# Preparing float64 weights: sign by a mask, remainders by an accumulating transfer, and a check for small weights

## The chip, the cores and the metric

One core of a Trainium2 chip runs the kernel. The metric is the device time of one execution in microseconds (us), less is better. The engines are PE (TensorE, with its weight loads, PEld), DVE (VectorE), ACT (ScalarE), POOL (GpSimd) and SP (SyncE, which here issues most transfers). Each engine runs its own list of instructions in order and waits on semaphores for the others.

## What is computed

A gated linear attention over 4 batches, 8 heads, 768 positions and a head width of 48, and on its output two matrix products with a piecewise quadratic between them:

```python
f = 1.0 / (1.0 + np.exp(-f_logit))
for t in range(S):
    state = f[:, :, t, :, None] * state + np.einsum('bhd,bhe->bhde', k[:, :, t], v[:, :, t])
    y[:, :, t] = np.einsum('bhd,bhde->bhe', q[:, :, t], state)
...
h = x @ w_in
g = np.where(pos, h, np.where(neg, 0.0, (h + beta) ** 2 / (4.0 * beta)))
return (g @ w_out).astype(np.float32)
```

x has 3072 rows and 384 columns, w_in is 384 by 2048 and w_out 2048 by 384. The two weight matrices arrive as float64; q, k, v and f_logit are float32.

## The kernel before

**Blocks.** The 768 positions are cut into NI = 6 row blocks of C = 128; with the 4 batches each block gives N = 512 columns to the products. The heads are taken in NP = 4 pairs. For each block and pair, `gate` makes running products of the forget gates (two scans on DVE), and `scores`, `outputs` and `states` make the attention by matmuls of the chunk and a state carried from block to block. `outputs` also splits its result into a rounded part (on ACT) and the remainder (on DVE), x; the fourth pair's part, y, reaches its place in x by six small transfers (`move`, x<-y in the profile).

**Units.** The products of a block are cut into NJ = 16 units of 128 columns of w_in. A unit is 9 matmuls in `mm_in` (L202), then act_1, act_2 on ACT, act_3 on DVE (L214), act_hi on ACT (L217, writes ghi), act_lo on DVE (L220, writes glo), and 9 matmuls in `mm_out` (L226). There are 96 units, numbered here from 0, so unit 16 is the first of the second block. Each product runs in three terms, of rounded parts and remainders: w_lo·hi, w_hi·hi and w_hi·lo.

**Weights.** They come as 24 pieces of 128 by 512 float64 (512 KB), in `order`: three pieces of w_in, three of w_out, and so on, as the first block's units need them; unit j of the first block needs the w_in pieces of its group of four units. The two 32-bit words of a number lie side by side in `raw`: lw and hw. `split_piece` shifts and joins them in `bits` to a float32 whose two highest bits are not yet right (L299, L302), reads the sign from the high word with two passes on ACT (L306, L307), takes the absolute value on ACT (L308), multiplies both on DVE (L309), rounds the result to w_hi on ACT (L311) and subtracts for w_lo on DVE (L312). There are four `raw` and two `bits` buffers. `outs`, where results are gathered for their transfer, lie in the `raw` buffers too.

**Order.** Nothing runs in program order: every piece of work is an `Op` with an engine, a cost from the table COST and what it depends on, and `Plan.order` simulates the engines to lay down one fixed order for each. At a moment it takes, of the work that is ready, what has the earliest latest start. A transfer issued by SP that has to wait holds every later one on SP's list. Where the plan sees PE idle for long, it puts in matmuls of zeros (`warm`, L280).

**The end.** A test of the first gates (ok, flag) decides whether a general path, slow and step by step, computes the whole again. With the inputs here it isn't taken.

Of the kernel before, what the change touches and what calls it, by code (L numbers as in the profile page):

```python
# [22 lines left out]
NI = S // C  # L23
# [4 lines left out]
N = B * C  # L28
HEADS = ((0, 48), (64, 112))

LEAST = 1e-15

NT = 3

W = 512
NW = DM * DF // (128 * W)
# [1 line left out]

HOP, LANDING, PER_KB, NEAR = 200, 2000, 3.0, 2000
COST = dict(mm=227, scores=1100, y0=1050, y=1850, states=500, turn=500, rows=317, scan=1145, dve=605, small=200, state=365,  # L40
            words=430, words2=690, act=710, copy=530, sig=540, issue=480, near=600, least=300)


class Op:
# [91 lines left out]
def gla_moe(ctx: ExitStack, tc: tile.TileContext, ff, kqd, f0, vv, wd, maskd, identd, gates, values, headsd, out):  # L136
    nc = tc.nc
    const = ctx.enter_context(tc.tile_pool(name="const", bufs=1))
# [3 lines left out]
    def tiles(count, shape, dtype, name):  # L142
        return [const.tile(shape, dtype, name=f"{name}_{k}") for k in range(count)]
# [7 lines left out]
    v = tiles(3, [C, B, 2, D], F32, "v")  # L151
# [27 lines left out]
    def wide(a):  # L179
        return a.rearrange("r b c -> r (b c)")  # L180
# [55 lines left out]
    add = plan.add  # L236

    def dma(dst, src, kb, *deps):
        return add("SP", "issue", lambda: nc.sync.dma_start(dst, src), *deps, kb=kb)
# [26 lines left out]

    def constants():
        nc.gpsimd.memset(ones_col, 1.0)
        for t, a in ((half, 0.5), (up, 512.0), (down, -512.0)):
            nc.gpsimd.memset(t, a)  # L270

    set_consts = add("POOL", 200, constants)
# [12 lines left out]
    piece = []  # L285
# [2 lines left out]
        order += [3 * q + n for n in range(3)] + [NW + 3 * q + n for n in range(3)]  # L288
    split = {}

    def split_piece(k):
        c = order[k]
        words = raw[k % 4].bitcast(U32).rearrange("p (n t) -> p n t", t=2)
        lw, hw = words[:, :, 0], words[:, :, 1]
        t = bits[k % 2]
        val, sign = t.bitcast(F32), hw.bitcast(F32)
        loaded = dma(raw[k % 4], wd[c], 8 * 128 * W / 1024, piece[k - 4] if k >= 4 else None)

        m = vec("words", lambda: nc.vector.tensor_scalar(  # L299
            out=t, in0=hw, scalar1=3, scalar2=0xC0000000, op0=ALU.logical_shift_left, op1=ALU.bitwise_xor),  # L300
            loaded, split[order[k - 2]] if k >= 2 else None)
        v = vec("dve", lambda: nc.vector.scalar_tensor_tensor(  # L302
            out=t, in0=lw, scalar=29, in1=t, op0=ALU.logical_shift_right, op1=ALU.bitwise_or), m)


        s = sca("words2", lambda: nc.scalar.activation(sign, sign, AF.Identity, bias=up), m, set_consts)  # L306
        s = sca("words2", lambda: nc.scalar.activation(sign, sign, AF.Sign, bias=down), s)  # L307
        v = sca("copy", lambda: nc.scalar.activation(val, val, AF.Abs), v)  # L308
        v = vec("dve", lambda: nc.vector.tensor_tensor(out=val, in0=val, in1=sign, op=ALU.mult), v, s)  # L309
        piece.append(v)  # L310
        h = sca("copy", lambda: nc.scalar.copy(w_hi[:, c], val), v)  # L311
        l = vec("dve", lambda: nc.vector.tensor_tensor(out=w_lo[:, c], in0=val, in1=w_hi[:, c].bitcast(F32), op=ALU.subtract), h)  # L312
        split[c] = [h, l]


    banks = {k: [] for k in range(6)}
# [217 lines left out]
        g["lo"] = vec("dve", lambda: act_lo(a, ghi[u % 2], glo[u % 2]), o, unit_out.get(u - 2))  # L534


    outs = [t.bitcast(F32)[:, 0:N] for t in raw[:3]]
    put = []

    def unit_2(u):  # L540
        i, j = divmod(u, NJ)
        hi, lo = ghi[u % 2], glo[u % 2]
        g = gs[u]
        need = [split[NW + c] for c in range(j * DM // W, ((j + 1) * DM - 1) // W + 1)]
        if j < NJ - 1:
            def first():
                mm_out(hi, lo, j, range(3), (0, 1))
                opened.update(bank=po[2], start=False)

            held = left.get(i - 1, [d for k in (3, 4, 5) for d in banks[k]]) if j == 0 else None  # L550
            add("PE", 6 * COST["mm"], first, g["hi"], need, held)
            unit_out[u] = add("PE", 3 * COST["mm"], lambda: mm_out(hi, lo, j, range(3), (2,)), g["lo"])
        else:
            left[i] = []
            for e in range(3):
                def last(e=e):
                    opened["bank"] = None
# [4 lines left out]
                o = (sca if e == 1 else vec)("dve", lambda e=e, t=t: copy_out(e, t), unit_out[u], put[-3] if len(put) >= 3 else [split[c] for c in order[-4:]])  # L562
                left[i].append(o)
                put.append(dma(out[i, :, e], t, 256, o))


    def prepare(n):
# [21 lines left out]
    for u in range(NI * NJ):  # L589
        unit_1(u)  # L590
        for kind, n in sorted(groups.get(u, [])):
            if kind == 0:
                prepare(n)
                if pairs[n][0] < NI - 1:
                    (transpose_tensor if pairs[n][0] < BY_TENSOR else transpose_rows)(n)
                scores(n)
            else:
                outputs(n)
                states(n)

        if 1 <= u < NI * NJ - 2:
            unit_2(u - 1)
    for u in range(NI * NJ - 3, NI * NJ):
        unit_2(u)

# [7 lines left out]
            o.emit()  # L613

    ok = const.tile([128, NI * NT * B + 1], F32, name="ok")
    nc.vector.tensor_scalar(out=ok[:, 1:], in0=f0s, scalar1=LEAST, scalar2=None, op0=ALU.is_ge)
    nc.vector.tensor_reduce(out=ok[:, 0:1], in_=ok[:, 1:], axis=mybir.AxisListType.X, op=ALU.min)
    ps = wide(pa[0])  # L620
    nc.tensor.matmul(ps[0:1, 0:1], ok[:, 0:1], ones_col, start=True, stop=True)
    flag = const.tile([1, 1], I32, name="flag")
    nc.vector.tensor_scalar(out=flag, in0=ps[0:1, 0:1], scalar1=127.5, scalar2=None, op0=ALU.is_lt)
    bad = nc.values_load(flag, min_val=0, max_val=1)
    with tc.If(bad > 0):
        heads = const.tile([R, 2], F32, name="heads")
        nc.sync.dma_start(heads, headsd)
        tmp = kq[:3]
# [115 lines left out]
```

## Time and profile before

| | us |
|---|---|
| median of 3 runs | 528.43 (527.32 to 530.09) |
| the profiled execution | 526.78, span 525.0 |
| granted TensorE clock, mean | 0.996 |
| PE / PEld busy | 505.8 / 404.8 |
| DVE busy | 386.0 |
| ACT busy | 274.4 |
| POOL busy | 11.9 |
| transfers | 41.67 MB, mean 79 GB/s |

The profile is of one execution. Its page gives the busy time of each engine, the span in 40 slices, the chain of work that ended last, and groups of instructions by line, engine, operation, tiles and shape, with their count, busy time, mean duration in ns, and the engine's idle time ahead of them with what ended it. A group reads "L299 DVE TENSOR_SCALAR bits<-raw 128x512 ... x24 | 10.0, 423 | 0.3": line 299, 24 instructions, 10.0 us, 423 ns each, 0.3 us idle ahead. In a timeline the first two numbers are the start and the duration in us. PE's busy time counts matmuls whose ends are modelled, so PE is not at its peak wherever it is called busy; its pace is read from the starts of its matmuls.

### The profile page before, as it was taken

Reading aid. Unit: us, or ns where it says so; the run is one execution under the profiler, and the core shown is the slowest. Engines: PE = TensorE matmul, PEld = TensorE weight load, DVE = VectorE, ACT = ScalarE, POOL = GpSimd, SP = SyncE. Lnnn points to the kernel's source line nnn. Section 1 sums busy time; section 2 is a strip of 40 time slices with the busy share of each in tenths; the row PEclk is TensorE's granted clock in tenths of the full one; section 3 lists DMA queues with packets and bytes.
Section 4 is the critical chain, followed back from the end, with each engine's and each line's share of the span. In section 5 each row is a group of like instructions: output and inputs, shape, how many; then the busy total and the mean of one; then the engine's idle time right before and its main releaser. Section 6 shows DMA issues by size and latency. Waiting matters only on the chain.

```text
span 525.0 us, 8314 instructions
## 1 busy us (share of the span) xinstructions
PE 505.8 (96%) x3245; PEld 404.8 (77%) x3253; DVE 386.0 (74%) x774; ACT 274.4 (52%) x447; POOL 11.9 (2%) x30
## 2 busy tenths in 40 slices
PE   8868999989999999999999999999999999999995
PEld 4546777868877778788888888888888888888884
DVE  7899999999999999997897698864544333433333
ACT  3578988986443444434534434434443444544442
POOL 1100000000000000000000000000000000000000
PEclk9989999999999999999999999999999999999999
DMA  8784454532322033222014112012200001100001
GB/s 294 252 295 140 138 190 151 186 117 46 100 76 66 2 95 87 70 60 73 21 56 96 60 57 77 1 55 63 66 24 1 1 0 32 61 1 0 1 0 64
DMA packets 17612, 41.67 MB, mean 79 GB/s; under 512 B 2976, under 2 KB 6560, under 8 KB 17568
## 3 DMA queue, kind: packets, MB, share of 16 engines
q1 hardware_dynamic: 16416, 38.73, 23.2%
q10 hardware_dynamic: 1152, 2.37, 1.9%
q8 instruction: 27, 0.44, 0.4%
q14 instruction: 17, 0.14, 0.1%
HBM read 31.63 MB, written 4.72 MB: 69 GB/s over the span
## 4 chain that ended last, share of the span: by engine, by line
PE 71%; DVE 21%; ACT 3%; issue 2%; DMA 1%; ACTq 0%; DVEq 0%
PE po L226 31%; PE ph L202 30%; PE pa L419 3%; PE pa L473 2%; PE pa L469 2%; DVE act L214 2%; DVE glo L220 2%; DVE kn L452 2%; DVE am L425 2%; DVE w_lo L312 2%; DVE bits L309 2%; DVE bits L302 2%; DVE bits L299 1%; DVE w L362 1%; DVE f L369 1%
## 5 line engine op out<-in xcount | busy, mean ns | idle before, releaser
L202 PE MATMUL ph<-x,w_hi 128*128 128x512 f32 x576 | 178.3, 391 | 0.0
L206 ACT ACTIVATE act<-ph,half 128x512 f32<-128x512 f32 x96 | 65.9, 687 | 132.7 <-PE ph L202 125.8
L202 PEld LDWEIGHTS ph<-x,w_hi 128*128 128x128 f32 x576 | 108.7, 189 | 22.9
L226 PE MATMUL po<-ghi,w_lo 128*128 128x512 f32 x288 | 116.2, 403 | 4.0 <-ACT ghi L217 4.0
L214 DVE SCALAR_TENSOR_TENSOR act<-ph,act 128x512 f32<-128x512 f32 x96 | 65.9, 686 | 69.6 <-ACT act L209 69.0
L202 PE MATMUL ph<-x,w_lo 128*128 128x512 f32 x288 | 113.4, 394 | 3.4 <-DMA x<-y 3.4
L226 PE MATMUL po<-ghi,w_hi 128*128 128x512 f32 x288 | 112.5, 390 | 0.0
L217 ACT CAST ghi<-act 128x512 fp32r<-128x512 f32 x96 | 59.5, 620 | 80.0 <-DVE act L214 79.8
L226 PE MATMUL po<-glo,w_hi 128*128 128x512 f32 x288 | 83.5, 391 | 0.5 <-DVE glo L220 0.5
L220 DVE TENSOR_TENSOR glo<-act,ghi 128x512 fp32r<-128x512 f32 x96 | 66.0, 687 | 24.1 <-ACT ghi L217 23.1
L226 PEld LDWEIGHTS po<-ghi,w_lo 128*128 128x128 f32 x288 | 54.0, 188 | 20.3 <-ACT ghi L217 7.7
L202 PEld LDWEIGHTS ph<-x,w_lo 128*128 128x128 f32 x288 | 54.4, 189 | 15.5 <-DMA x<-y 3.9
L226 PEld LDWEIGHTS po<-glo,w_hi 128*128 128x128 f32 x288 | 53.6, 188 | 13.5 <-DVE glo L220 2.3
L209 ACT ACTIVATE act<-act 128x512 f32<-128x512 f32 x96 | 60.7, 632 | 2.8
L226 PEld LDWEIGHTS po<-ghi,w_hi 128*128 128x128 f32 x288 | 54.1, 188 | 10.3
L452 DVE STREAM_TRANSPOSE kn<-kq 32x128 f32<-32x128 f32 x192 | 58.1, 303 | 2.9
L425 DVE TENSOR_TENSOR am<-pa,mask 128x512 f32<-128x512 f32 x43 | 29.4, 686 | 19.3 <-PE pa L419 15.1
L468 PE MATMUL pa<-am,v 128*64 128x128 f32 x184 | 35.5, 279 | 1.1 <-DVE am L425 0.6
L469 PE MATMUL pa<-am,v 128*48 128x128 f32 x184 | 34.5, 277 | 0.5 <-DVE am L425 0.5
L472 PE MATMUL pa<-kq,dbd 112*64 112x128 f32 x160 | 30.6, 272 | 0.0
L473 PE MATMUL pa<-kq,dbd 112*48 112x128 f32 x160 | 30.6, 272 | 0.0
L419 PEld LDWEIGHTS pa<-kq 48*128 48x128 f32 x344 | 21.3, 187 | 6.6 <-issue 5.6
(79 smaller groups left out, 478.5 us busy)
## 6 DMA issues: line engine op xcount, KB each, us to landing
raw<-in_w SPq DMA_DIRECT2D x24, 512.0 KB, 4.4
kq<-in_kq SPq DMA_DIRECT2D x18, 512.0 KB, 3.7
v<-in_v SPq DMA_DIRECT2D x24, 192.0 KB, 4.0
out_y<-raw SPq DMA_DIRECT2D x18, 256.0 KB, 2.2
f<-in_f SPq DMA_DIRECT2D x16, 256.5 KB, 2.7
kq<-kq SPq DMA_DIRECT2D x18, 64.2 KB, 2.3
kq<-kq ACTq DMA_DIRECT2D x18, 64.2 KB, 2.7
x<-y SPq DMA_DIRECT2D x18, 64.0 KB, 3.6
```

The source lines that it names most:

```text
L202: nc.tensor.matmul(ps, w_in(part, j, kt), xt[:, kt, t], start=(n == 0), stop=(n == 8))
L206: nc.scalar.activation(a, ps, AF.Relu, bias=half, scale=0.5)
L209: nc.scalar.activation(a, a, AF.Square)
L214: nc.vector.scalar_tensor_tensor(out=a, in0=ps, scalar=1.0, in1=a, op0=ALU.max, op1=ALU.min)
L217: nc.scalar.copy(hi, a)
L220: nc.vector.tensor_tensor(out=lo, in0=a, in1=hi.bitcast(F32), op=ALU.subtract)
L226: nc.tensor.matmul(po[e], w_out(part, j, e), g, start=(j == 0 and n == 0), stop=(j == NJ - 1 and n == 2))
L419: nc.tensor.matmul(ps[:, b], kt[a:z, B - 1 - b], qt[a:z, b], start=True, stop=True)
L425: o = vec("dve", lambda t=t, ps=ps: nc.vector.tensor_tensor(out=t, in0=ps, in1=mask.rearrange("u (o t) -> u o t", o=1).broadcast_to([C, B, ...
L452: nc.vector.transpose(kn[n % 2][u:u + 32, :, r:r + 32], src[:, :, u:u + 32])
L469: nc.tensor.matmul(ps[64:R, m], vb[:, D:], ms[1][:, m], start=True, stop=first)
L473: nc.tensor.matmul(ps[64:R, m], dt[:, m, 64:R], qt[:, m], start=False, stop=True)
```

## The change

A piece is now put together with three DVE instructions: shift and mask (so that the two highest bits are zero), join with the low word, join with the two highest bits of the high word. That gives the float32 at once, with its sign, for a weight in float32's range; one too small for it comes out wrong (SMALL, 2^-15, is the bound for the high word when that is read as a float32). The two sign passes, the absolute value and the multiplication go. ACT writes w_lo as minus the rounded value, and POOL issues a transfer that adds the value to it in place: w_lo is the remainder. w_hi is made as before. `raw` has three buffers, `bits` four.

For such weights, `small_piece` loads all 24 pieces a second time into the third `raw` buffer, one after the other, and reduces each to its least absolute high word (DVE, into ok). `test` joins that with the test of the first gates, inside the plan and ahead of the last three units' second halves, and the general path, if taken, splits the weights again with the old sign. The results' buffers, `outs`, move into the first two `raw` buffers. COST gains the issue on POOL and loses the sign pass.

```diff
-    raw = tiles(4, [128, W], I64, "raw")
-    bits = tiles(2, [128, W], U32, "bits")
+    raw = tiles(3, [128, W], I64, "raw")
+    bits = tiles(4, [128, W], U32, "bits")
...
     def split_piece(k):
+
         c = order[k]
...
-        loaded = dma(raw[k % 4], wd[c], 8 * 128 * W / 1024, piece[k - 4] if k >= 4 else None)
+        loaded = dma(raw[k % 3], wd[c], 8 * 128 * W / 1024, piece[k - 3] if k >= 3 else None)
+
 
         m = vec("words", lambda: nc.vector.tensor_scalar(
-            out=t, in0=hw, scalar1=3, scalar2=0xC0000000, op0=ALU.logical_shift_left, op1=ALU.bitwise_xor),
-            loaded, split[order[k - 2]] if k >= 2 else None)
+            out=t, in0=hw, scalar1=3, scalar2=0x3FFFFFF8, op0=ALU.logical_shift_left, op1=ALU.bitwise_and),
+            loaded, split[order[k - 4]] if k >= 4 else None)
         v = vec("dve", lambda: nc.vector.scalar_tensor_tensor(
             out=t, in0=lw, scalar=29, in1=t, op0=ALU.logical_shift_right, op1=ALU.bitwise_or), m)
-
-
-        s = sca("words2", lambda: nc.scalar.activation(sign, sign, AF.Identity, bias=up), m, set_consts)
-        s = sca("words2", lambda: nc.scalar.activation(sign, sign, AF.Sign, bias=down), s)
-        v = sca("copy", lambda: nc.scalar.activation(val, val, AF.Abs), v)
-        v = vec("dve", lambda: nc.vector.tensor_tensor(out=val, in0=val, in1=sign, op=ALU.mult), v, s)
+        v = vec("dve", lambda: nc.vector.scalar_tensor_tensor(
+            out=t, in0=hw, scalar=0xC0000000, in1=t, op0=ALU.bitwise_and, op1=ALU.bitwise_or), v)
         piece.append(v)
+
+        n = sca("copy", lambda: nc.scalar.activation(w_lo[:, c], val, AF.Copy, scale=-1.0), v)
+        l = add("POOL", "swdge", lambda: nc.gpsimd.dma_start(w_lo[:, c], val, accum_op=ALU.add), n, near=True)
         h = sca("copy", lambda: nc.scalar.copy(w_hi[:, c], val), v)
-        l = vec("dve", lambda: nc.vector.tensor_tensor(out=w_lo[:, c], in0=val, in1=w_hi[:, c].bitcast(F32), op=ALU.subtract), h)
         split[c] = [h, l]
+
+    seen = []
+
+    def small_piece(c):
+
+        loaded = dma(raw[2], wd[c], 8 * 128 * W / 1024, seen[-1:] or piece[-3:])
+        seen.append(vec("dve", lambda: nc.vector.tensor_reduce(
+            out=ok[:, 1 + NG + c:2 + NG + c], in_=words_of(raw[2])[1].bitcast(F32), axis=mybir.AxisListType.X, op=ALU.min,
+            apply_absolute_value=True), loaded))
...
-    outs = [t.bitcast(F32)[:, 0:N] for t in raw[:3]]
+    outs = [raw[0].bitcast(F32)[:, 0:N], raw[0].bitcast(F32)[:, N:2 * N], raw[1].bitcast(F32)[:, 0:N]]
...
+    def test():
+        def compare():
+            nc.vector.tensor_scalar(out=ok[:, 1:1 + NG], in0=f0s, scalar1=LEAST, scalar2=None, op0=ALU.is_ge)
+            nc.vector.tensor_scalar(out=ok[:, 1 + NG:], in0=ok[:, 1 + NG:], scalar1=SMALL, scalar2=None, op0=ALU.is_ge)
+            nc.vector.tensor_reduce(out=ok[:, 0:1], in_=ok[:, 1:], axis=mybir.AxisListType.X, op=ALU.min)
+
+        ps = wide(pa[0])
+        o = vec(500, compare, seen, [c["pf"] for c in gates_of])
+        o = add("PE", 500, lambda: nc.tensor.matmul(ps[0:1, 0:1], ok[:, 0:1], ones_col, start=True, stop=True), o, banks[0], set_consts)
+        vec("small", lambda: nc.vector.tensor_scalar(out=flag, in0=ps[0:1, 0:1], scalar1=127.5, scalar2=None, op0=ALU.is_lt), o)
...
     for k in range(2 * NW):
         split_piece(k)
+    for c in range(2 * NW):
+        small_piece(c)
```

The plan lays down a new order. In what follows the lines of the changed kernel have numbers of their own: L306, L309 and L311 are the three instructions of a piece, L216 and L222 are act_3 and act_lo, L512 is the remainder of x or y, L325 the reduction.

DVE's list just ahead of the first unit, before the change. L299, L302, L309 and L312 belong to pieces, L425 masks scores, L481 on y is what the x<-y transfers of the first block wait for:

```order
L481 TENSOR_TENSOR x_88<-pa_110,x_88 112x512
L309 TENSOR_TENSOR bits_100<-bits_100,raw_96 128x512
L425 TENSOR_TENSOR am_78<-po_115,mask 128x512
L425 TENSOR_TENSOR am_79<-po_116,mask 128x512
L309 TENSOR_TENSOR bits_99<-bits_99,raw_97 128x512
L312 TENSOR_TENSOR w_lo<-bits_100,w_hi 128x512
L299 TENSOR_SCALAR bits_100<-raw_98 128x512
L302 SCALAR_TENSOR_TENSOR bits_100<-raw_98,bits_100 128x512
L312 TENSOR_TENSOR w_lo<-bits_99,w_hi 128x512
L481 TENSOR_TENSOR y_90<-po_117,y_90 112x512
```

The same place in the changed kernel, from the end of the third piece on; the gate's scans are w (L393) and f (L400):

```order
L311 SCALAR_TENSOR_TENSOR bits_100<-raw_97,bits_100 128x512
L512 TENSOR_TENSOR x_88<-pa_111,x_88 112x512
L393 SCALAR_TENSOR_TENSOR w<-f_66,ones 128x512
L456 TENSOR_TENSOR am_78<-po_116,mask 128x512
L456 TENSOR_TENSOR am_79<-po_117,mask 128x512
L306 TENSOR_SCALAR bits_101<-raw_95 128x512
L309 SCALAR_TENSOR_TENSOR bits_101<-raw_95,bits_101 128x512
L311 SCALAR_TENSOR_TENSOR bits_101<-raw_95,bits_101 128x512
L396 TENSOR_SCALAR end_77<-w 128x4
L399 RECIPROCAL rec<-end_77 128x4
L400 SCALAR_TENSOR_TENSOR f_66<-f_66,rec 128x512
L512 TENSOR_TENSOR y_90<-po_118,y_90 112x512
```

A fourth piece stood ahead of y's remainder in both. It came with a `raw` buffer of its own (raw_98) and now comes with the first one's (raw_95), and the next gate's two scans have moved ahead of y's remainder.

SP's list at that time, before; the first four pieces' loads are already issued, and raw_95 is the fifth piece's:

```order
L239 DMA kq_68<-in_kq 128x1024
L244 DMA kq_71<-kq_69 16x1028
L244 DMA kq_71<-kq_70 16x1028
L239 DMA v_73<-in_v 128x384
L239 DMA kq_69<-in_kq 128x1024
L239 DMA raw_95<-in_w 128x512
L239 DMA kq_70<-in_kq 128x1024
```

And now, where raw_95 is the fourth piece's:

```order
L241 DMA kq_68<-in_kq 128x1024
L246 DMA kq_71<-kq_69 16x1028
L246 DMA kq_71<-kq_70 16x1028
L241 DMA v_73<-in_v 128x384
L241 DMA kq_69<-in_kq 128x1024
L241 DMA raw_95<-in_w 128x512
L241 DMA kq_70<-in_kq 128x1024
L241 DMA raw_96<-in_w 128x512
L241 DMA raw_97<-in_w 128x512
```

The load of the first buffer's second piece stands where it stood, behind the kq load, but it is the fourth piece's now. Two more loads (raw_96, raw_97) follow behind the next kq load, ahead of a v load that stood ahead of them.

DVE's list some 60 units later in the changed kernel, where the checks stand (nothing of the kind stood there before):

```order
L216 SCALAR_TENSOR_TENSOR act_86<-ph_114,act_86 128x512
L222 TENSOR_TENSOR glo_93<-act_86,ghi_91 128x512
L325 TENSOR_REDUCE ok<-raw_97 128x1
L216 SCALAR_TENSOR_TENSOR act_87<-ph_115,act_87 128x512
L222 TENSOR_TENSOR glo_94<-act_87,ghi_92 128x512
L325 TENSOR_REDUCE ok<-raw_97 128x1
L216 SCALAR_TENSOR_TENSOR act_86<-ph_114,act_86 128x512
L222 TENSOR_TENSOR glo_93<-act_86,ghi_91 128x512
L325 TENSOR_REDUCE ok<-raw_97 128x1
L216 SCALAR_TENSOR_TENSOR act_87<-ph_115,act_87 128x512
```

A reduction (L325) stands ahead of each of three act_3 (L216) here, and waits there for its load. The 24 reductions stand between the act_3 of unit 31 and that of unit 74; stretches with one per unit are up to six units long and hold a pair of the attention.

More of the change, by code (lines that the diff above doesn't have):

```diff
@@ L31 @@
 LEAST = 1e-15
+SMALL = 2.0 ** -15
 NT = 3
@@ L268, in constants @@
         nc.gpsimd.memset(ones_col, 1.0)
-        for t, a in ((half, 0.5), (up, 512.0), (down, -512.0)):
+        for t, a in ((half, 0.5), (up, 768.0), (down, -768.0)):
             nc.gpsimd.memset(t, a)
@@ new lines, in split_again @@
+    def split_again(c):
+        lw, hw = words_of(raw[0])
+        t = bits[0]
+        val, sign = t.bitcast(F32), hw.bitcast(F32)
+        nc.sync.dma_start(raw[0], wd[c])
+        nc.vector.tensor_scalar(out=t, in0=hw, scalar1=3, scalar2=0x3FFFFFF8, op0=ALU.logical_shift_left, op1=ALU.bitwise_and)
+        nc.vector.scalar_tensor_tensor(out=t, in0=lw, scalar=29, in1=t, op0=ALU.logical_shift_right, op1=ALU.bitwise_or)
+        nc.vector.scalar_tensor_tensor(out=t, in0=hw, scalar=0xC0000000, in1=t, op0=ALU.bitwise_and, op1=ALU.bitwise_or)
+        nc.scalar.activation(sign, sign, AF.Identity, bias=up)
+        nc.scalar.activation(sign, sign, AF.Sign, bias=down)
+        for _ in range(2):
+            nc.vector.tensor_tensor(out=val, in0=val, in1=sign, op=ALU.mult)
+        nc.scalar.copy(w_hi[:, c], val)
+        nc.vector.tensor_tensor(out=w_lo[:, c], in0=val, in1=w_hi[:, c].bitcast(F32), op=ALU.subtract)
@@ L602, in gla_moe @@
             unit_2(u - 1)
+    test()
     for u in range(NI * NJ - 3, NI * NJ):
@@ L613, in gla_moe @@
             o.emit()
[L617 to L623, printed above, removed]
     bad = nc.values_load(flag, min_val=0, max_val=1)
     with tc.If(bad > 0):
+        for c in range(2 * NW):
+            split_again(c)
         heads = const.tile([R, 2], F32, name="heads")
```

17 lines of the change are left out of this document (11 added, 6 removed).

## The prediction

> **What bounds the kernel now.** The first view is the page's engine table with its slices, which says where to look and not what bounds: PE is called busy throughout, but its ends are modelled.
>
> ```profile
> span 525.0 us, 8314 instructions
> ...
> PE   8868999989999999999999999999999999999995
> ...
> DVE  7899999999999999997897698864544333433333
> ```
>
> VectorE (DVE) is full for the first half and a third full at the end. The windows by stage come next.
>
> ```profile
> 37.00:120.00 83.00, 78.59 (x495) 60.61 (x499) 80.90 (x148) 73.89 (x127) 1.53 (x3) 0.98 0.47 152
> 120.00:220.00 100.00, 98.66 (x670) 80.03 (x670) 96.56 (x220) 46.66 (x75) 3.52 (x6) 1.00 0.24 64
> 220.00:345.00 125.00, 125.00 (x890) 104.22 (x889) 105.16 (x234) 55.10 (x87) 1.80 (x5) 1.00 0.20 59
> ```
>
> Behind the span stand PE, weight loads, DVE, ACT and POOL in us, the granted clock, the DMA share and GB/s. From 37 to 120 us DVE works 80.90 of 83.00 us. The chain of waits, cut to that window, agrees:
>
> ```profile
> by line: DVE bits L309 10.3%; DVE w_lo L312 9.7%; DVE bits L302 9.5%; issue 8.9%; DVE act L214 7.8%; DVE glo L220 7.7%; PE ph L202 7.2%; DVE bits L299 6.8%; DVE am L425 5.8%; DVE f L369 3.0%; PE po L226 2.8%; DVE dbd L404 2.4%; DVE w L362 2
> ...
> 47.44 1.19 DVE bits L309 x2
> 48.62 0.60 DVE glo L220
> ```
>
> The four weight lines lead it, and the last rows give the price of a full-width DVE instruction on that chain: 0.60 us from one to the next, though the groups call it 0.69 long. So this stage is bound by VectorE. How much could a free VectorE give? PE's own rate stands in the chain later on:
>
> ```profile
> 260.80 1.09 PE pa L419 x16
> ...
> 264.16 2.26 PE po L226 x9
> 266.42 2.04 PE ph L202 x9
> ...
> 513.18 6.34 PE po L226 x27
> ```
>
> Nine matmuls take 2.04 us, a unit (18) 4.08, and 96 units 391.7. An attention pair takes 264.16 − 260.80 = 3.36, with the slower restart of 0.22 behind it 3.6; 20 pairs are 72. The first unit starts at 36.96 (row below): 36.96 + 391.7 + 72 = 500.7, and PE ends at 513.18 + 6.34 = 519.52. So 18.8 us are lost behind 36.96, and no VectorE saving can give more. They are lost early: unit 16, the first of the second row block, has its act_3 here,
>
> ```profile
> 138.99 0.69 DVE L214 SCALAR_TENSOR_TENSOR act<-ph,act 128x512 f32<-128x512 f32 x1
> ```
>
> while PE alone would have done the 32 groups of nine and the four pairs ahead of it, their transposes included, by about 36.96 + 65.3 + 16.6 = 119, and ScalarE another 2 us later.
>
> **The change, part by part.**
>
> ```profile
> L299 DVE TENSOR_SCALAR bits<-raw 128x512 uint32<-128x512 uint32 x24 | 10.0, 423 | 0.3
> L302 DVE SCALAR_TENSOR_TENSOR bits<-raw,bits 128x512 uint32<-128x512 uint32 x24 | 16.3, 688 | 0.4
> L309 DVE TENSOR_TENSOR bits<-bits,raw 128x512 f32<-128x512 f32 x24 | 15.9, 681 | 0.0
> L312 DVE TENSOR_TENSOR w_lo<-bits,w_hi 128x512 fp32r<-128x512 f32 x24 | 16.1, 684 | 1.1 <-ACT w_hi L311 1.1
> L306 ACT ACTIVATE raw<-raw,up 128x512 f32<-128x512 f32 x24 | 18.3, 770 | 1.0 <-DVE bits L299 1.0
> L307 ACT ACTIVATE raw<-raw,down 128x512 f32<-128x512 f32 x24 | 18.2, 772 | 0.5
> L308 ACT ACTIVATE bits<-bits 128x512 f32<-128x512 f32 x24 | 14.4, 622 | 2.0 <-issue 2.0
> L311 ACT CAST w_hi<-bits 128x512 fp32r<-128x512 f32 x24 | 14.5, 617 | 1.1 <-DVE bits L309 1.0
> ```
>
> *VectorE per piece.* L299 and L302 stay, L309 and L312 go, and a second instruction of L302's form comes: four become three, 2.48 us become 1.80. The one saved is worth 0.60 on the chain, 24 pieces 14.4 us. In both orders all 24 pieces stand ahead of unit 16's act_3, so the whole saving falls into the bound stage; but the new order also puts about 1.1 us of other VectorE work ahead of that act_3: 13.3 us remain. If VectorE were not the bound for part of the stage, less; the cap above is the other end. ScalarE loses L306, L307 and L308 and gains one pass of L311's length: 2.16 − 0.62 = 1.55 us a piece less. None of its lines is among those that the chain names; I count nothing.
>
> *Three raw buffers for four.* The fourth piece now waits for the first one's third instruction. The start shows what that does:
>
> ```profile
> 19.26 0.42 DVE L299 TENSOR_SCALAR bits<-raw 128x512 uint32<-128x512 uint32 x1
> 19.71 0.69 DVE L302 SCALAR_TENSOR_TENSOR bits<-raw,bits 128x512 uint32<-128x512 uint32 x1
> ...
> 31.46 0.69 DVE L481 TENSOR_TENSOR y<-po,y 112x512 fp32r<-112x512 f32 x1
> ...
> 24.98 0.33 SPq L239 DMA_DIRECT2D kq<-in_kq  x1
> 25.37 0.42 SPq L239 DMA_DIRECT2D raw<-in_w  x1
> ...
> 36.96 0.79 PE L202 MATMUL ph<-x,w_lo 128*128 128x512 f32 x1 [3.41 <-DMA x<-y]
> ...
> raw<-in_w SPq DMA_DIRECT2D x24, 512.0 KB, 4.4
> kq<-in_kq SPq DMA_DIRECT2D x18, 512.0 KB, 3.7
> out_y<-raw SPq DMA_DIRECT2D x18, 256.0 KB, 2.2
> ...
> DMA to landing us min/median/max: 2.0/3.5/7.3
> ```
>
> From 19.26 on the new order has, before the fourth piece, three instructions of L299's form at 19.71 − 19.26 = 0.45, eleven full-width ones at 0.60 and a scan of twice that: 9.2 us, so VectorE reaches it near 28.4. Its load is behind the kq load in SP's queue, so it is issued at about 25.4 and lands 4.4 later, at 29.8: a wait of 1.4 us (0 to 3.7 with landings of 2.0 to 7.3, raw's and out_y's together). Behind it stand 1.65 us of piece and 1.6 of the next gate, then y's remainder, which the x<-y transfers and so the first unit wait for: it starts at about 33.1 instead of 31.46. Cost 1.6. For later pieces, VectorE's own work between a buffer's release and its reuse sums, by these prices, in the new order to 4.6 to 13 us, against 4.4 of landing; in the old order, with four, to 7.6 and more. Six of the later reuses lie under 6 us, where a second load in flight makes a short wait: 1.5 us, 0 to 5.
>
> *The remainder by ScalarE and an accumulating transfer.* No row shows such a transfer. From below it costs out_y's 2.2 us (256 KB), from above raw's worst, 7.3. It reads two arrays of 256 KB and writes one, so I take the 512 KB row, 4.4. POOL's issue lies between SP's 0.33 and the longest POOL copy, 1.18:
>
> ```profile
> 13.98 1.18 POOL L380 COPY f0s<-kq 128x4 f32<-128x4 f32 x1 [10.87 <-DVE kq L378]
> ...
> L380 POOL COPY f0s<-kq 128x4 f32<-128x4 f32 x18 | 9.3, 522 | 336.1 <-DVE kq L378 336.1
> ```
>
> With ScalarE's 0.62 the chain is about 6 us. Two covers hide it: the units need a piece some two units (8 us) behind its last VectorE instruction, and with four bits buffers the reuse lies 6.2 to 16.5 us of VectorE work away. Cost 0; if transfers took 7.3 us, about 2. POOL's copies of first gates wait behind them, and nothing waits for those but the test at the end.
>
> *The check.* 24 loads of 512 KB and 24 reductions come between units 31 and 73. No row has a reduction 512 wide; one of 72 takes 0.23, the slowest full-width instruction, the scan, twice the 0.60. I take 0.69, as the others of this width. They cost nothing where act_3 has room:
>
> ```profile
> L619 DVE TENSOR_REDUCE ok<-ok 128x1 f32<-128x72 f32 x1 | 0.2, 231 | 0.0
> ...
> 505.13 0.62 ACT L217 CAST ghi<-act 128x512 fp32r<-128x512 f32 x1 [0.76 <-DVE act L214]
> ...
> 506.90 0.39 PE L226 MATMUL po<-ghi,w_lo 128*128 128x512 f32 x1
> ```
>
> ghi is ready at 505.75 and used at 506.90: 1.15 us of room per unit, more than one reduction ahead of act_3. Each load waits in SP's queue for the reduction before it, with x<-y, kq and f loads behind it: 3.7 + 0.69 + some 0.1 is 4.5 us a check, and the order spaces them at a unit, 4.08, with a pair's 3.36 in each longer run. Cost 0.5; without that cover 24 × 0.60 = 14. The test's one matmul moves towards the end and is one matmul either way: 0.
>
> *Sum.* −13.3 + 1.6 + 1.5 + 0 + 0.5 = −9.7 us against this execution's 526.78 (span 525.0 and 1.8 around it): 517.1. This execution lies 1.65 under the median of the runs shown, 528.43, so the forecast there is 518.7.
>
> **The rivals.** *The queue of POOL and VectorE hold each other up.* L299 takes 423 ns where its neighbours of the same width take 688, so it runs in a faster form, and POOL has next to nothing to do today (3 rows in 83 us), so no row shows the two side by side for long. If each of the 24 L299 waited for one issue of POOL, of 0.52 like the mean of its copies, the gain would shrink by 12.5 us, to 531; where half of them collide, to 525. For it speaks that both engines are packed into the same 80 us; against it that even today's copies beside DVE last 0.5 us. The Trainium skill, "SBUF — State Buffer", sections "Who interferes with whom" and "Summary: rules for kernel authors", has this as a rule: a VectorE instruction in a two-port mode and GpSimd shut each other out for its whole length, and it advises against hiding a transfer issued by GpSimd under VectorE work; no run here shows it yet.
>
> *Slower: the accumulating transfers land late.* A bits buffer is held from L306 to the landing: about 4 us of piece, 1 of ScalarE, then the transfer, L. Four buffers pass 24 pieces in 24 × (5 + L) / 4 us. The old pieces ran as these rows say,
>
> ```profile
> L299 DVE TENSOR_SCALAR bits<-raw x24: 416/422/429, 19.3 to 120.7; 128x512 uint32<-128x512 uint32 x24
> ...
> L312 DVE TENSOR_TENSOR w_lo<-bits,w_hi x24: 670/685/694, 24.3 to 126.4; 128x512 fp32r<-128x512 f32 x24
> ```
>
> from 19.3 to 127: 108 us. So it decides from L = 13 on; at L = 15 the stage takes 120 us, 12 more than before: 540. For it speaks that the transfer is of an unseen kind, in a stage with a DMA share of 0.47 already; against it every landing seen is under 7.3.
>
> *PE becomes the bound.* If VectorE has less in front of the units than summed, since ScalarE's relief also ends its waits, all of the 18.8 but the late start of 1.6 is gained: 528.4 − 17.2 = 511.2. For it speaks that ScalarE too works 73.89 of 83 us; against it that VectorE's sum puts unit 16's act_3 near 130, well behind PE's 121.
>
> *It doesn't do what it says.* With three buffers every reuse could be late: if all 21 came at the smallest distance, 4.6, and loads took 5.2 (raw's 4.4 and a share for a second one in flight), each would wait 0.6, 12 us together, and the saving goes into waits: 526 to 530. For it speaks that the loads now share the stage with 24 more transfers.
>
> **How the numbers follow.** Forecast 0.55; PE the bound 0.10; POOL and VectorE in each other's way, 522 to 531, 0.12, of which half is still faster; late transfers 0.13; the saving given back 0.10, where a little of it is faster too. Half a per cent (525.8 to 531.1) is about what a measurement of this kernel tells from no change. Faster 0.73 (0.55 + 0.10 + 0.06 + 0.02), same 0.12, slower 0.15. The range asked for takes in the PE bound below and the collisions above: 511 to 527, with the late transfers left out; the forecast's own, from the bounds of its terms, is 514 to 524.
>
> **What would show it.** Right: unit 16's first act_3 about 9 us earlier than 139, VectorE still 95% busy between 38 and 110, the first unit a little later than 36.96, PE without gaps afterwards. Waits of bits on raw of over 5 us in sum, or of bits on w_lo's transfer, would show the loads or the transfers as the new bound; L299's successor longer than 0.43 the collisions; gaps of PE between units 31 and 73 the check.

## The result and the profile after

| | before | after |
|---|---|---|
| median of 20 runs each, us | 529.01 (525.32 to 532.0) | 528.66 (526.98 to 530.6) |
| ratio of times, 95% interval | | 1.0 (0.9979 to 1.002) |
| the profiled execution, us | 526.78, span 525.0 | 527.07, span 525.3 |
| granted TensorE clock, mean | 0.996 | 0.986 |
| first unit starts, us | 36.96 | 44.72 |
| unit 16's act_3, us | 138.99 | 136.46 |
| transfers, MB | 41.67 | 60.57 |

The change made no difference that can be measured; 518.7 us was forecast. The first page of the profile after, with the two rows of slices that were shown of before:

```profile
span 525.3 us, 8288 instructions
...
PE   8765998999999999999999999999999999999995
...
DVE  7866998999999999898898798865655443433332
```

PE has a dent in the fourth slice that it did not have, and VectorE has lost work in the third and the fourth. The chain of waits after, cut to the first units (start, length, what), names the dent:

```profile
33.40 0.59 DVE y L512
34.01 10.57 DMA x<-y
44.72 6.90 PE ph L204 x18
```

y's remainder is made at 33.40, near where the forecast put it (33.1). Then 10.57 us pass until the first of y's small transfers that the unit needs has landed. Before, it was some 4.8: from the end of y's remainder, 32.15, to 36.96. The windows by stage after (behind the span PE, weight loads, DVE, ACT and POOL in us, the clock, the DMA share, GB/s):

```profile
37.00:120.00 83.00, 72.35 (x467) 59.34 (x468) 73.68 (x134) 51.85 (x91) 17.56 (x22) 0.94 0.90 232
120.00:220.00 100.00, 99.48 (x674) 80.78 (x674) 96.11 (x218) 44.31 (x72) 3.60 (x7) 1.00 0.27 76
220.00:345.00 125.00, 125.00 (x889) 104.22 (x889) 108.26 (x237) 55.12 (x87) 1.80 (x5) 1.00 0.30 93
```

From 37 to 120 us VectorE worked 7 us less and PE 6 less too: VectorE, busy for 80.90 of 83 us before, is no longer full, so something else holds it. The DMA share stands at 0.90 where it was 0.47. Finer windows, first of before, then of after:

```profile
25.00:36.00 11.00, 7.74 (x80) 4.55 (x76) 10.76 (x19) 8.65 (x16) 0.00 (x0) 1.00 0.89 308
36.00:46.00 10.00, 7.09 (x24) 5.44 (x25) 8.87 (x17) 7.98 (x15) 0.00 (x0) 0.83 0.47 145
```

```profile
25.00:36.00 11.00, 9.02 (x90) 5.21 (x89) 8.93 (x16) 6.45 (x14) 3.61 (x4) 1.00 0.95 278
36.00:46.00 10.00, 1.28 (x3) 1.13 (x4) 6.09 (x11) 2.18 (x4) 1.72 (x2) 0.69 1.02 233
```

Before, the transfer engines were already 0.89 busy up to 36 us, and then they came free. After, they stay full. The row of POOL's queue, q0, for 36 to 46 us (packets, MB, share of the engines) says by what, and SP's list shows what stands ahead of x<-y:

```profile
q0 software_dynamic: 482, 0.86, 49.2%
```

```profile
31.87 0.33 SPq L241 DMA_DIRECT2D raw<-in_w  x1
33.05 0.33 SPq L241 DMA_DIRECT2D v<-in_v  x1
34.01 4.98 SPq L246 DMA_DIRECT2D x<-y  x3
```

POOL's queue took half of the engines' time there. The raw load issued at 31.87 landed 12.3 us later, at 44.1, the v load at 44.4 and the first x<-y of SP's list at 44.6. Before, the raw load ahead of x<-y was issued at 29.18 and landed at 36.4, x<-y at 36.6. In the traces of all the kernels of this document the first x<-y of SP's list lands 0.2 to 0.5 us behind the load just ahead of it. So x<-y is late because the loads ahead of it are late; no run moved it elsewhere.

The waits after (engine and line, what for: us, times, longest) and the rows of the queues:

```profile
PE ph L204 <- DMA x<-y: 9.4, 1, 9.4
DVE bits L306 <- DMA raw<-in_w: 8.6, 5, 2.3
ACT w_lo L315 <- DMA x<-y: 7.9, 1, 7.9
...
DVE ok L325 <- DMA raw<-in_w: 2.3, 2, 1.5
```

```profile
q0 software_dynamic: 3456, 6.29, 6.8%
...
w_lo<-bits POOLq DMA_DIRECT2D x24, 256.0 KB, 6.9
```

ScalarE's 7.9 us are the issue of x<-y: it issues three of the six, the last at 40.93 (33.63 before), and does nothing else meanwhile. POOL's queue q0 holds the 24 accumulating transfers. They landed after 6.9 us (median; 3.5 to 11.6), where 4.4 had been taken, and used 6.8% of all 16 transfer engines' time over the span: 35.7 us, 1.5 each. They were issued between 25.7 and 120.4 us.

### The profile page after: what moved, and what is told of

Same layout as the page of the kernel before. It is cut to its first block, busy times and chain, and to the rows that moved or that the text cites. A ratio compares the mean times of both kernels' runs of the same rounds, so it can differ in the third digit from the quotient of the medians.

```text
span 525.3 us, 8288 instructions
## 1 busy us (share of the span) xinstructions
PE 500.1 (95%) x3226; PEld 404.0 (77%) x3226; DVE 387.3 (74%) x775; ACT 243.6 (46%) x399; POOL 30.8 (6%) x54
## 2 busy tenths in 40 slices
DMA packets 24526, 60.57 MB, mean 115 GB/s; under 512 B 3744, under 2 KB 7328, under 8 KB 24480
## 3 DMA queue, kind: packets, MB, share of 16 engines
q0 software_dynamic: 3456, 6.29, 6.8%
## 4 chain that ended last, share of the span: by engine, by line
PE 71%; DVE 17%; DMA 7%; issue 2%; ACT 2%; ACTq 0%; SPq 0%; DVEq 0%
PE po L228 31%; PE ph L204 30%; DMA f<-in_f 3%; PE pa L450 3%; DMA x<-y 2%; PE pa L504 2%; PE pa L500 2%; DVE glo L222 2%; DVE kn L483 2%; DVE am L456 2%; DVE w L393 2%; DVE act L216 2%; DVE bits L311 1%; DVE f L400 1%; DMA raw<-in_w 1%
## 5 line engine op out<-in xcount | busy, mean ns | idle before, releaser
L216 DVE SCALAR_TENSOR_TENSOR act<-ph,act 128x512 f32<-128x512 f32 x96 | 65.8, 686 | 64.7 <-ACT act L211 63.6
L222 DVE TENSOR_TENSOR glo<-act,ghi 128x512 fp32r<-128x512 f32 x96 | 65.9, 686 | 22.3 <-ACT ghi L219 21.2
L228 PEld LDWEIGHTS po<-ghi,w_hi 128*128 128x128 f32 x288 | 54.1, 188 | 10.4
L456 DVE TENSOR_TENSOR am<-pa,mask 128x512 f32<-128x512 f32 x43 | 29.3, 685 | 17.6 <-PE pa L450 13.9
```

The costliest lines, as they stand in the source:

```text
L216: nc.vector.scalar_tensor_tensor(out=a, in0=ps, scalar=1.0, in1=a, op0=ALU.max, op1=ALU.min)
L222: nc.vector.tensor_tensor(out=lo, in0=a, in1=hi.bitcast(F32), op=ALU.subtract)
L228: nc.tensor.matmul(po[e], w_out(part, j, e), g, start=(j == 0 and n == 0), stop=(j == NJ - 1 and n == 2))
L456: o = vec("dve", lambda t=t, ps=ps: nc.vector.tensor_tensor(out=t, in0=ps, in1=mask.rearrange("u (o t) -> u o t", o=1).broadcast_to([C, B, ...
```

## The experiments

The theory, called **jam**: the accumulating transfers crowd the others, x<-y and so the first unit, then the loads. The rivals: **raw**, the waits of three raw buffers; **port**, POOL and VectorE in each other's way; **other bound**, that VectorE's instructions were not the limit in the first place. The table holds all runs, the sections take them in groups. The medians are of 4 to 12 executions, and each ratio is to executions of the kernel before at the same time. "First" is the start of the first unit and "unit 16" its act_3, both from the profiled execution (that of the run with twelve pieces lies 1% above its median, and nothing is read from it).

| run | median us | ratio to before (95%) | first | unit 16 |
|---|---|---|---|---|
| VectorE subtracts all | 529.78 | 1.0017 (0.9998 to 1.0036) | 38.45 | 140.0 |
| VectorE subtracts 6 | 540.05 | 1.0186 (1.0149 to 1.0223) | 39.78 | 153.2 |
| four raw, three bits | 539.43 | 1.021 (1.0169 to 1.025) | 45.72 | 148.2 |
| POOL subtracts | 533.38 | 1.0095 (1.007 to 1.012) | 39.04 | 141.7 |
| plain transfers | 524.8 | 0.9943 (0.9921 to 0.9965) | 41.35 | 132.6 |
| 6, price 8 us | 524.02 | 0.9924 (0.99 to 0.9947) | 39.56 | 134.1 |
| 12, price 8 us | 525.64 | 0.9938 (0.991 to 0.9967) | | |
| no check | 528.23 | 1.0008 (0.9988 to 1.0028) | 44.54 | 136.3 |
| before, extra transfers | 543.5 | 1.0283 (1.0254 to 1.0311) | 54.55 | 156.7 |
| all, price 7 us | 530.04 | 1.0041 (1.0022 to 1.0059) | 42.48 | 136.4 |
| 3, price 8 us | 531.84 | 1.0049 (1.0025 to 1.0074) | 46.08 | 141.4 |
| 6, price 5 us | 529.63 | 1.0018 (0.9996 to 1.004) | 37.40 | 140.7 |
| 16 columns | 519.34 | 0.9836 (0.9806 to 0.9866) | 39.63 | 128.0 |
| 256 columns | 522.98 | 0.9905 (0.9873 to 0.9937) | 41.13 | 130.8 |

### Without the accumulating transfers, VectorE subtracts again

```diff
-        n = sca("copy", lambda: nc.scalar.activation(w_lo[:, c], val, AF.Copy, scale=-1.0), v)
-        l = add("POOL", "swdge", lambda: nc.gpsimd.dma_start(w_lo[:, c], val, accum_op=ALU.add), n, near=True)
         h = sca("copy", lambda: nc.scalar.copy(w_hi[:, c], val), v)
+        l = vec("dve", lambda: nc.vector.tensor_tensor(out=w_lo[:, c], in0=val, in1=w_hi[:, c].bitcast(F32), op=ALU.subtract), h)
```

> The changed kernel with w_lo made by a VectorE subtraction for all 24 pieces, so no accumulating transfer; three raw buffers, the short joining of bits and the check stay. Jam theory (the accumulating transfers fill the DMA engines from 25 to 45 us and make x<-y, and so the first unit, 8.6 us late): x<-y lands in under 5.5 us, the first unit starts at 37 to 39 us in place of 44.7, the waits of bits on raw fall from 8.6 us to under 3; VectorE has four instructions a piece as in the kernel before, so the time is 526 to 530. Raw theory (three raw buffers are what is short): the waits on raw stay near 8 us and the time is 532 to 537.

x<-y took 3.57 us, the first unit started at 38.45, and the time is that of before. So the jam goes with the transfers; and with the same three raw buffers no instruction at L306 waits for raw any more (8.6 us in the change). It also shows that three raw buffers, the check and ScalarE's relief (232.4 us busy for 274.4) come to a net loss of 2 us at most (the interval's upper end), and that with four VectorE instructions a piece again there is nothing to gain.

The second kernel does this for the first six pieces alone (`if k < 6:` in front of the new lines, `else:` in front of the old).

> The changed kernel with the VectorE subtraction for the first six pieces and the accumulating transfer for the other 18. Jam theory: the first unit starts at 37 to 39.5 us, six more VectorE instructions cost 3.6 us of the 13 saved, the time is 520 to 525. Raw theory: the first unit may be earlier but later waits on raw take it back, 526 to 530. Other-bound theory (something that both kernels share ends last by unit 18, where their act_3 meet, so an earlier first unit is worth nothing): 527 to 530.

The first unit came at 39.78, a little behind the 37 to 39.5 of the jam theory, but the time was 540, outside of all three expectations. The waits of this run, and three rows of its chain:

```profile
PEld ph L204 <- DMA w_lo<-bits: 10.4, 8, 2.0
...
PE ph L204 <- DMA w_lo<-bits: 6.7, 8, 1.6
```

```profile
55.04 7.87 DMA w_lo<-bits
78.35 9.28 DMA w_lo<-bits
...
118.80 7.61 DMA w_lo<-bits
```

Now PE itself stands and waits for the remainders. The plan reckons 2 us for such a landing (NEAR) and lays the pieces just ahead of their use; the three of these rows need 7.6 to 9.3. In the change as it is PE hardly waits for them, perhaps because its first unit is late; that was not tried by itself.

### Four raw buffers, three bits buffers

```diff
-    raw = tiles(3, [128, W], I64, "raw")
-    bits = tiles(4, [128, W], U32, "bits")
+    raw = tiles(4, [128, W], I64, "raw")
+    bits = tiles(3, [128, W], U32, "bits")
...
-        loaded = dma(raw[k % 3], wd[c], 8 * 128 * W / 1024, piece[k - 3] if k >= 3 else None)
+        loaded = dma(raw[k % 4], wd[c], 8 * 128 * W / 1024, piece[k - 4] if k >= 4 else None)
```

(The zeros of `warm` are cut to 256 columns to make room.)

> The changed kernel with four raw buffers and three bits buffers (the zeros for the idle matmuls are read twice, to make room). Jam theory: x<-y still takes about 10 us, the first unit starts at 42 to 46, the time is 526 to 532. Raw theory: the waits of bits on raw go, the fourth piece no longer holds up y, the first unit starts by 41 and the time is 520 to 525.

The first unit is as late as the jam theory said (45.72), but 539 us lie outside of both expectations. VectorE's waits at L306 in this run:

```profile
  DMA w_lo<-bits: 13.4, 6
  DMA raw<-in_w: 5.9, 2
```

With one bits buffer fewer, VectorE waits for the landings themselves: 13.4 us, where the change, with four, has no such wait. So this run does not tell what a fourth raw buffer is worth by itself; it tells that the first unit is late with four of them too.

### POOL subtracts

```diff
+        l = add("POOL", 1100, lambda: nc.gpsimd.tensor_tensor(out=w_lo[:, c], in0=val, in1=w_hi[:, c].bitcast(F32), op=ALU.subtract), h)
```

> The changed kernel with w_lo made by a subtraction on POOL for all 24 pieces: no accumulating transfer, no negated copy on ScalarE, three VectorE instructions a piece. Jam theory: the first unit starts at 37 to 39.5 and the VectorE saving shows in the time: 516 to 521. Port theory (POOL and VectorE hold each other up when both read SBUF): VectorE's instructions with two inputs grow from 0.69 to 0.8 us and more where they meet, the time is 523 to 530. Other-bound theory: 527 to 530.

The first unit started at 39.04, without the jam, and yet the kernel was slower than before, by more than even the port theory allowed. POOL's group in this run, then one line of VectorE in it and that line after the change, with minimum, median and maximum in ns:

```profile
L316 POOL TENSOR_TENSOR w_lo<-bits,w_hi 128x512 fp32r<-128x512 f32 x24 | 39.7, 1667 | 54.7 <-ACT w_hi L315 54.7
```

```profile
L309 DVE SCALAR_TENSOR_TENSOR bits<-raw,bits x24: 675/692/1782, 20.5 to 122.6; 128x512 uint32<-128x512 uint32 x24
```

```profile
L309 DVE SCALAR_TENSOR_TENSOR bits<-raw,bits x24: 682/691/694, 21.3 to 117.5; 128x512 uint32<-128x512 uint32 x24
```

Beside a subtraction on POOL a VectorE instruction takes up to 1.78 us for 0.69 (L306, with its one array, up to 1.47 for 0.42); VectorE is busy 404.9 us for 387.3. Beside POOL's issues of transfers in the change (24 of 0.86 us) L309 takes what it takes alone. L306 met such an issue four times and took 0.55 and 0.53 us in two of them: 0.2 us in sum.

### Is it the adding, the order's price, or the check?

Plain transfers: `accum_op=ALU.add` left out, so that w_lo holds the value and not the remainder; every order on VectorE, ScalarE and SyncE is that of the change.

> The 24 transfers from bits to w_lo stay with their place, size and queue, but copy instead of adding (w_lo then holds the value, not the remainder). If the adding is what is slow: they land after 2 to 4 us instead of 6.9, x<-y of the first block takes under 6 us, the first unit starts at 37 to 39.5, 515 to 522 us. If every transfer that POOL issues is that slow: 5.5 to 7.5 us, the first unit at 42 to 46, 526 to 531.

In between: 524.8 us, landings of 5.6, x<-y 7.20. Same bytes, same queue, and the queue's row tells what the adding costs:

```profile
q0 software_dynamic: 3456, 6.29, 4.0%
```

4.0% for 6.8%: the adding takes 1.7 times the transfer engines' time of a copy, and without it unit 16's act_3 comes 3.9 us earlier (132.6 against 136.5). But the copies jam too.

The plan's price: `NEAR * o.near`, and 4 (8 us), 3.5 or 2.5 for the accumulating transfers.

> As the run with VectorE's subtraction for the first six pieces, but the plan is told 8 us for the landing of an accumulating transfer instead of 2. If that run lost its time because the order brings pieces just in time for a landing of 2 us: PE waits for w_lo under 3 us in sum (22 there), the first unit starts at 37 to 40, 518 to 524 us. If the transfers cannot be carried that fast in this stage, whatever the order: PE's and VectorE's waits for them stay above 12 us, 530 to 541.

> The same price of 8 us, with VectorE's subtraction for the first twelve pieces. VectorE has 7.2 us less to save than with none. If order and the transfers of the first block's start are what costs: 519 to 526 us and no wait of PE for w_lo. If the transfers themselves: 528 to 536.

> The change as it is, all 24 transfers accumulating, with the plan told 7 us for a landing instead of 2. If the order's wrong price costs something beside the jam at the start: the first unit still at 42 to 46, and 522 to 526 us. If all of the loss is traffic: 526 to 531.

> Price of 8 us, VectorE's subtraction for the first three pieces. If the jam ahead of the first unit is made by the transfers of those that land between 25 and 44 us, two of them are left: the first unit at 39 to 43, 523 to 528.

> VectorE's subtraction for the first six pieces, price of 5 us. With 2 us 540, with 8 us 524. If the order needs only to be near the truth (6.9): 522 to 527. If 524 was a lucky order: anything, 520 to 540.

With six pieces on VectorE and 8 us, PE's weight loads wait 0.3 us for w_lo (10.4 with 2 us) and the time is 524.02, faster than both kernels: 4.5 us under before. With twelve, 525.64. With 5 us, they are back (PEld 9.7, PE 7.1 us) and the time is 529.63, not the 522 to 527 expected of a price that is nearly true. With three pieces the first unit is late again (46.08) and the time 531.84, both above what was expected. With all 24 transfers the price alone gave nothing: 530.04. Its profiled execution, at 526.16, was the fastest of its runs. With six pieces the price counts for up to 16 us (540, 530, 524 with 2, 5 and 8 us), but each price makes another order, and those differ by several us; these runs do not give the price a value of its own, and 524 may be a lucky order.

Without the check (the 24 second loads, reductions, and their test left out):

> Leaves out the 24 second loads, their reductions and their part of the test. If the check is hidden as forecast (0.5 us): 526.5 to 529.5 us, act_3 of units 31 to 73 as far apart as with it. If loads or reductions hold the stream up: 518 to 525.

528.23 against 528.66: nothing that can be told apart, as forecast.

### The kernel before, with extra transfers

```diff
         split[c] = [h, l]
+        if k + 6 < 2 * NW:
+            ahead = w_lo[:, order[k + 6]].bitcast(F32)
+            spared[k + 6] = add("POOL", 1000, lambda: nc.gpsimd.dma_start(ahead, ones.rearrange("p b c -> p (b c)"), accum_op=ALU.add), h, set_ones, set_spare[k], near=True)
```

(POOL clears the 18 parts of w_lo at the start.)

> The kernel before, with its order on VectorE, ScalarE and SyncE, plus 18 accumulating transfers of 256 KB that POOL issues behind pieces 0 to 17. They add a constant to a part of w_lo that a later piece overwrites, so nothing waits for them but that piece, six further on. If they slow the other transfers of the stage: x<-y of the first block 7 to 11 us instead of 4.5, the first unit at 40 to 45 instead of 37, the DMA share from 36 to 46 us over 0.85 instead of 0.47, 531 to 538 us. If the loss of the change comes from the waits on its own buffers and not from the traffic: first unit at 37 to 38, 527 to 530.

```profile
39.04 0.61 DVE y L486
39.66 14.75 DMA x<-y
54.42 0.14 issue
54.55 5.64 PE ph L202 x17
```

The traffic alone, with the order on VectorE, ScalarE and SyncE unchanged, makes x<-y 10 us longer, and the DMA share from 36 to 46 us is 1.09. x<-y and the time lie beyond what was expected (7 to 11 us, and 531 to 538 us). The kernel is not as clean as it was meant to be: since nothing holds these transfers back, POOL issued nine of them in one burst, more than the change does, so the run shows the direction and not the size; and the 7 us by which y is late are another matter (last section). What the first unit was late, 17.6 us, was still there at the last unit.

### The change, with the bytes taken out

```diff
-nc.gpsimd.dma_start(w_lo[:, c], val, accum_op=ALU.add)
+nc.gpsimd.dma_start(w_lo[:, c, 0:16], val[:, 0:16], accum_op=ALU.add)
```

> The change with every order as it is; each accumulating transfer carries 16 of the 512 columns (8 KB for 256 KB), so w_lo keeps minus the rounded value in the other columns. If the traffic of these transfers took the whole gain: x<-y of the first block 4 to 6 us, the first unit at 37 to 39.5, unit 16's act_3 at 126 to 130, 517 to 521 us. If the order (other work ahead of units 17 and 18) and the three raw buffers took a part of it: the first unit as early, but 521.5 to 526 us.

> The same with 256 of the 512 columns (128 KB). If the loss grows with the bytes carried: the first unit half-way between the run with 16 columns and the change (near 41), and so the time, half-way too. If it is a fixed cost of such a transfer and not of its bytes: as the change, first unit at 43 to 46, 526 to 530 us.

Every order on VectorE, ScalarE and SyncE is kept, and w_lo is not the remainder in these two. The chain with 16 columns:

```profile
32.97 0.59 DVE y L512
33.58 5.96 DMA x<-y
39.63 5.98 PE ph L204 x18
```

519.34 us, where the forecast for the whole change was 518.7; with half of the bytes 522.98, with all 528.66. (The first unit, at 39.63, is 0.1 us later than the first case allowed.) POOL still issues its 24 transfers, of 0.86 us each; only the bytes are gone. This settles it: the bytes of the accumulating transfers cost some 9 us (9.3 by the medians, 8.7 by the ratios to before), and without them the time is what was forecast. The first half costs 3.6 and the second 5.7; with four executions of each run, that difference is not clear of the noise.

## Why the prediction was wrong

The starts of act_3 (VectorE's timeline) show where it went, all but the first column with the order of the change:

| unit | before | after | plain | 256 columns | 16 columns |
|---|---|---|---|---|---|
| 0 | 42.0 | 50.6 | 46.8 | 46.8 | 45.0 |
| 8 | 89.7 | 92.1 | 87.7 | 87.0 | 84.5 |
| 16 | 139.0 | 136.5 | 132.6 | 130.8 | 128.0 |
| 18 | 147.7 | 148.1 | 144.2 | 142.4 | 139.6 |
| 32 | 218.1 | 217.2 | 213.1 | 212.3 | 208.5 |
| 95 | 514.6 | 513.9 | 510.3 | 509.1 | 505.8 |

- **The step that failed: "The remainder by ScalarE and an accumulating transfer ... Cost 0".** It asked who waits for w_lo, found two covers, and they held in the change: no VectorE instruction waited for it, PE for 0.4 us, and the first unit waited longer for x<-y. It did not ask what else the transfer engines had to carry. They slowed SP's loads, and x<-y stands behind these at the start, with nothing to cover it: 5.1 of the loss (44.72 against 39.63 with 16 columns; the raw load ahead of x<-y takes 12.3 us to land for 7.0). From there to unit 16 3.4 more went (91.7 against 88.3 us). In that stretch VectorE waited 2.8 us for raw (none with 16 columns), and the first 18 matmuls took 6.90 us for 5.98, with a granted clock of 0.61 for 0.71 over them; how the 3.4 divides was not tried. The row that spoke against it could have been read: a DMA share of 0.89 between 25 and 36 us; the prediction used only the stage's mean, 0.47 from 37 on. The landing itself was 6.9 in the median, inside the bounds of 2.2 to 7.3, and for 7.3 the prediction had counted "about 2": the transfer's length was the wrong measure, its share of the engines the right one. The sign that the prediction named, waits of bits on raw of over 5 us in sum, came (8.6).
- **VectorE, −13.3: right, if the bytes are taken out.** The first and the third of the three instructions that a piece has now:

```profile
L306 DVE TENSOR_SCALAR bits<-raw x24: 400/424/548, 20.9 to 117.0; 128x512 uint32<-128x512 uint32 x24
...
L311 DVE SCALAR_TENSOR_TENSOR bits<-raw,bits x24: 678/685/693, 24.1 to 118.7; 128x512 uint32<-128x512 uint32 x24
```

  From the first unit to unit 16's act_3, 102.0 us before, it took 88.3 with 16 columns: 13.7 less, and 10.3 less even with all the traffic. Forecast for that stretch were −13.3 and +1.5, 11.8 less. That VectorE was the bound is shown by the first run beside this one: four instructions again, the time of before again (529.78 against 519.34).
- **Right in the stage, too much at the end.** Of the 11.0 us by which unit 16 is earlier with 16 columns, 8.1 are left at unit 18: the new order has 22 VectorE instructions between the two act_3, the old 13. The prediction read its saving off at unit 16 and took it as final. That its sum (−9.7) came so near the measured loss of some 9 is partly chance: by its terms unit 16 was to be 10.2 earlier (it writes "about 9") and was 11.0, then 2.9 went, and 0.8 came back behind unit 18.
- **Three raw buffers, +1.6 and +1.5: near in size, by luck.** The fourth piece was to wait for its load until 29.8. The load came then (29.7), but VectorE reached the piece only at 29.97 and did not wait: it was 1.6 us late from the first piece on (20.88 for 19.26), after a wait of 1.53 for ScalarE's x in the new order. (From the prediction's own numbers, the upper bound of that wait is 4.3 and not 3.7.) Nor is y's remainder what sets the first unit, as the landings above show. With 16 columns the unit starts 2.7 later than before: the raw load ahead of x<-y is issued at 31.44 (29.18 before) and lands at 38.4 (36.4), a v load behind it at 38.9, and only then x<-y, at 39.3. VectorE waits 1.3 us for raw there, all of it ahead of the first unit; the rest of the 8.6 in the change is the traffic's.
- **The check, +0.5.** Right as far as can be told: from unit 32's act_3 to unit 72's 198.9 us before, 199.6 after, 200.2 without the check, and no gain in the time without it.
- **Late accumulating transfers: the right transfers**, with the wrong bound. It let them decide from 13 us on, by way of the bits buffers. In the change no instruction of VectorE waited for one; with three bits buffers VectorE waited 13.4 us for them, and in the run with six subtractions PE did. The price it gave, slower by 12, is what those two showed (540), not the change.
- **POOL and VectorE hold each other up: hardly, for issues; yes, for arithmetic** (L306 and L309 above). The Trainium skill, "SBUF — State Buffer", section "Who interferes with whom", says that a VectorE instruction with two inputs in SBUF contends with a GpSimd instruction that reads SBUF. By that rule L309, which reads raw and bits, is held up by POOL's subtraction, and the trace agrees: up to 1.78 us for 0.69. The advice of the same page, section "Summary: rules for kernel authors", against hiding a transfer issued by GpSimd under VectorE work, had next to no price here: 0.2 us of L306, where the rival had reckoned 12.5.
- **PE the bound**, 511, did not come up, not even with 16 columns. **The saving given back through late loads** has the right end, no change (526 to 530), and named the 24 more transfers as what speaks for it; VectorE did wait 8.6 us for raw, where it had reckoned 12. What it lacks is the larger part, x<-y behind the loads, and the short reuse distance of the raw buffers that it rested on costs 1.3 us without the traffic.

## What to carry to other kernels

A transfer that nobody waits for still takes its share of the transfer engines from those that somebody waits for: price it by its time on all the engines, against the DMA share of the very stretch in which it runs, and look for the small critical transfer behind it, and for the loads that stand ahead of that in its queue. Taking the bytes out and keeping the order is a cheap test that shows what such a stage is worth without them. A planner that is told a landing a third of the true one lays work just in time for a moment that does not come, as with six pieces on VectorE. This one makes the prediction's omission too: `Plan.order` adds up the other transfers on one `wire`, and a transfer marked near takes no time on it. A truer landing alone, with all 24 transfers, gained nothing.

## What the runs showed of the hardware

- An accumulating transfer of 256 KB in SBUF takes 1.7 times the engines' time of a plain one (6.8% for 4.0% of the span, 6.29 MB each), and its issue on POOL 0.86 us instead of 0.53. Accumulating transfers of 8, 128 and 256 KB, 24 of each, took 1.2, 4.0 and 6.8%: a fixed part, and one that grows with the bytes.
- A small VectorE instruction stood until a row of POOL's writes was over. In the run with extra transfers POOL cleared w_lo in a row of memsets that ended at 11.46 us, and two instructions of VectorE, of 128 by 2 numbers, stood from 4.71 to 11.48; before, they took 0.29. That run's timelines of POOL and VectorE:

```profile
7.22 4.24 POOL L291 MEMSET w_lo<- 128x512 f32 x9
```

```profile
4.71 6.77 DVE L370 TENSOR_SCALAR end<-w 128x2 f32<-128x2 f32 x2
```

  The two scans ahead of them ran beside the same memsets in their usual time (1.28 for the two). That the memsets held the two instructions is read from the ends, 11.46 and 11.48; no run tried it by itself.
